# A written-out matmul order made anew on a plan that also counts GpSimd and the readiness of split weights: one adaLN transformer block on one Trainium2 core

## The chip, the cores and the metric

The kernel runs on one core of one Trainium2 chip. The metric is the device time of one execution in microseconds (us); for the kernel before it is 2359.66 us, the median of three executions.

The engines are named as in the profile: PE is TensorE (PEld its weight loads), DVE is VectorE, ACT is ScalarE, POOL is GpSimd, SP is SyncE, which here issues all DMAs (SPq in the rows).

## The reference

One transformer block over a sequence of 2048 rows of 576 numbers, 32 heads of 18, feed-forward width 4608, all in fp32. Six vectors of 576 come from a conditioning vector `c`:

```python
mod = (silu(c) @ w_mod).reshape(1, 6, 1, -1)          # sa, ca, ga, sb, cb, gb
h = layernorm(x) * (1 + ca) + sa
q, k, v = heads(h @ wqkv)
p = softmax(q @ k.T * 18 ** -0.5)
x = x + ga * ((p @ v) @ wo)
h = layernorm(x) * (1 + cb) + sb
x = x + gb * (silu(h @ w1) @ w2)
```

## The kernel before

**Arithmetic.** Each fp32 factor of a projection is split into a high part and a low part, both in a rounded fp32 type that TensorE takes in one pass. A product is then three products: high by high, high by low, low by high (`PASS`). Activations are split as they are made; the weights `wqkv`, `wo`, `w1`, `w2` are split once. Splitting costs a copy (the high part, `w[:, 1]` in `split_half`, L728) and a subtraction (the low part, `w[:, 0]`, L744), both on GpSimd, and for `wo` and `w2` a multiplication by the gate `ga` or `gb` before it (L740).

**Stages.** A first part (scheduled by the class `Start`, not touched here) normalises x and makes the first queries, keys and values. Then comes the attention loop over four query blocks of 512 rows (`NQB`), each with eight groups of four heads ("quads"), each quad with 64 *slots*. One slot is two matmuls that share the PE array, one in each half of its rows: `psa` (L851), whose row maxima DVE takes (L853, the tile `mx`), and `psb` (L903), whose exponential ACT takes (L905, the tile `pt`). `psa` runs 40 double slots ahead of `psb` (`LEAD`), since the maxima have to be there. After the slots of 128 keys follow the value products `psv` (L940), eight matmul records of the trace for each such step. There are 2048 slots and 512 value steps in all.

**Fill.** Whatever else PE has to do is put between slots as *fill*, piece by piece (class `Filler`). While query block 0 runs, fill is the rest of the query and key projections (`psqk`, L632). When the last value step of block b is through, `post(b)` (L1007) makes the fill that runs beside the slots of block b+1:

- the output projection `psp`, four row tiles of 56 matmuls (lines L513 and L519), with the attention output split into `th` and `tl` (`o_T`, L1024 to L1032) as one factor and the split `wo` as the other;
- the addition to x (`add_x1`, L1053 on DVE, L1056 and L1057 by way of ACT and GpSimd) and the second layer norm (L1063 to L1081, with a power on GpSimd at L421);
- the transposes `psT` of the normalised rows `ob` (`h_T`, L1091), followed by ACT (`etmp`, L439), DVE (`hh`, L442) and GpSimd (`hl`, L446);
- 36 tiles of `w1` in 18 pairs (`mlp1`, 54 matmuls a pair: `ps<-hh,w1t`, `ps<-hl,w1t`), the SiLU (L1181 to L1191, whose low part `g` is made on GpSimd), and 36 tiles of `w2` in 9 rounds of four (`mlp2`, 192 matmuls a round: `ps<-w2t,g`), with another `add_x1`.

For b = 0 the weights of `post` are loaded raw and split as they are needed, in halves of a tile: `load_half` (L717) issues the DMA into one of three buffers `raw`, `split_half` (L728) issues the GpSimd work, and a finished tile is stored to DRAM, from where blocks 1 to 3 load it split. For b = 3 there are no more slots, and the fill runs alone.

**What sets the order.** PE's instructions stand in the order in which the program issues them; the other engines' order is made by the compiler's own scheduler, except that some instructions (`after_pe`, L491) are tied to the latest `psb`: among them the `raw` loads and the first instruction of each split. PE's order is the string `ORDER`, one letter a decision: `s` is a slot, `f` one piece of fill, a digit so many value steps. The main loop (L1650 on) reads it beside a plan of time (class `Plan`, L133): `plan.t` is the time at which PE is thought to be, `plan.op` puts an operation on a queue of ACT ("A") or DVE ("V") with a length in ns, `chain` a row of them, and `plan.ring`, `take` and `when` say when a PSUM buffer is thought free. Where the next letter is not yet possible by the plan, the plan's clock moves on by 20 ns and nothing is issued. So the plan doesn't wait on the chip: it only decides at which letter the loads, splits and layer-norm steps are issued, and which orders are possible at all. Three modes of PE are told apart in it (`half`: slots and fill in halves of the rows; `full`; `values`), with a charge for each change of mode.

GpSimd has no queue in this plan. What waits for it is guessed: the low parts of the attention output by a time (`o["th"]`, at + 1500), the low part of the SiLU by at + 1600, the normalised rows by at + 900, the readiness of split weights not at all: `proj`, `mlp1` and `mlp2` only ask for two free PSUM buffers (`pair_need`, L462). A `raw` load is issued when fewer than three halves are waiting to be split (`serve`, L753).

Of the kernel before, what the change touches and what calls it, by code (L numbers as in the profile page):

```python
# [25 lines left out]
KT = 5  # L26
# [14 lines left out]
CH = 4  # L41
# [20 lines left out]
    "sssfsssfsssfsss1sss1sssfsssfsssfss1sss1sss1sss1sss1sss1sss1sss2sssfsssfsssfsss1sss1sss1sss1ss1sssfsss2sssffsss"  # L62
    "1sssfsssfsssfsss1sss1sss1sss1sss1sss2sssffsssfsss1sss1sss1sss1sss1ss1sssfsss11sssffsss1sssfsssfsssfsss1sss1sss"
    "1sss1sss1ss1sssfsssffsss1sss1sss1sss1sss1sss1ss1sss1sssffffsssffsssfsssfsss1sss1sss1sss1sss1sss1sss1ss1sss1sss"
    "fffsssfsss1sss1sss1sss1sssf1sss1sssfsssffsss1sss2sssffsssfsssfsss1sss1sss1sss1sss1sss1ssffsssffsss1sss1sss1sss"
    "1sss1sssfffsssfsss1sss1sssf1sssfffsss1sss1sss1sss1sss1sssfffsssfsss1sss1sss1sss2sss1sssf1sss1sss1sssfsssfsssfs"
    "ss1sssfsss2sssffsss1sss1sss1sss1sss1ssfsssfsssfsss1sss1sss1ss2sssfsssfsssfsss1sss1sss1sss1sssfsss2sssffsss1sss"
    "1sss1sssfsssfsss1sss1sss1ssssfss1ss1ss1ss1ss1ssssssssssss1ss1ss1ss1fss1fss1ss1ssss1ssssssfffs1ssffsfsffffssfff"
    "sffffssffsfffffsfffffffss1fffffffssfffffffss1fffffffsfffffffss13sfffssffs1sffssffsfsffssffsfsfsfsffs3sfsfffsfs"
    "ffsfsfsfsfsfsffs2sfsfsffsfsffssffsfsfsfsfsfs13ssffsffssffsfsfs1ssffsffssffsfsfs1ssffsffssffsffss2ssffsffssffsf"  # L70
    "fss3ssffsfsfsfsffssffsfsfsfsffs3sfffsfsfsffssffsfsfsfsffs4sffsffssffsffss1ssffsffssffsffss21ssffsffssffsffss1s"
    "sffsffssffsfsfs2ssffsfsfsfsffssffsfsfsfsffss4ssffsfsfsfsffssffsfsfsfsfsfs1sfsfff3ssffsffss1ssffsffssffsfsfs1ss"
    "ffsffssffsffss2ssffsffssffsfsfs3ssffsfsfsfsffssffsfsfsfsfsfs13ssffsfsfsfsffssffsfsfsfsfsfs1sffffssfffsfs1sfsff"
    "fssffsffs3ssffsffssffsffss1sfsfsffssffsffss3ssffsfsfsfsffssffsfsffsffs3sfsfsffsfsffssffsfsfsfsffs4sfsfsffssffs"
    "fsfs1ssffsffssffsfsfs1sfsfffssffsffss2sfsfsffssffsffss3ssffsfsfsfsffssffsfsfsffsfs4ssffsfsfsfsffssffsfsfsfsfsf"
    "s22ssffffssffsffss1ssffsffssffsffss1ssffsffssffsfsfs1sfsfffssffsffss4ssffsfsfsfsffssffsfsfsfsffss3ssfffssffsff"
    "ssffsfsfsfsfsfs22ssffsffssffsffss1ssffsffssffsfsfs12ssffsffssffsffss1sfsfffssffsffs2ssffsfsfsfsffssffsfsfsfsff"
    "ss3ssfffssffsffssffsfsfsfsffss4ssffsffssffsfsfs1ssffsffssffsfsfs3ssffsffssffsffss1ssffsffssffsffss1ssffsfsfsfs"
    "ffss1sfsfss2ss1ss1ss1sffff1ffffsfsfsfsfs1ssffsffssffsfsfs1ssfffsfsffsfs1ssfffsfsffsfs1ssffsffssffsffss1fffffff"
    "ssfffffffss1fffffffssfffffffss1fffffffssfffffff1sffsffssffffss2sff2fs1ssffsfffsffssffsfsfsfsffs2sfsfsffsfsffss"  # L80
    "ffsfsfsfsfsfs3ssfffssffsffssffsfsfsfsfsfs13ssffffssffsffss1ssffsffssffsffss2ssffsffssffsffss1ssffffssffsfsfs3s"
    "sffsfsfsfsffssffsfsfsfsfsfs3ssfffssffsffssffsfsfsfsfsfs4ssffsffssffsffss1ssffsffssffsfsfs1ssffsffssffsfsfs4ssf"
# [26 lines left out]
GP = [range(i, i + 2) for i in range(0, 28, 2)]  # L109
MMC = 228  # L110
MMH = 131

TS, TV, TX, TL, TR = 228, 858, 100, 430, 60
TMAX, TEXP = 605, 495
TLAT = {"A": 100, "V": 85}


def head_rows(h):

    kt, r0 = divmod(DH * h, P)  # L120
    n = min(P - r0, DH)
# [252 lines left out]
def tile_adaln_block(ctx: ExitStack, tc: tile.TileContext, x, wqkv, wo, w1, w2, c, wfirst, wcol, out):  # L374
# [331 lines left out]
    def weights(key, make, n, src, scr, first, gate=None, hold=None):  # L706

        if not first:
            nc.sync.dma_start(f(make()), f(scr))
            return  # L710
# [1016 lines left out]
```

## Time and profile before

| | |
|---|---|
| time, median of 3 (lowest to highest) | 2359.66 us (2354.22 to 2360.62) |
| the profiled execution: its own time | 2358.8 us |
| its span, first to last instruction | 2356.2 us |
| first `psb` of query block 0, 1, 2, 3 | 155.8, 546.0, 1070.5, 1572.6 us |
| end of the last `psb` | 2077.4 us |
| PE busy | 2286.8 us |
| DVE busy | 1775.4 us |
| POOL busy | 711.9 us |

How to read it: the profile shows one execution. Its own time is 2.6 us more than its span, and 0.9 us less than the median. The rows of the table with `psb` say in which stretch of the span a query block's slots run: `post(0)`, with the splitting of `wo`, `w1` and `w2`, runs from 546 to about 1070 us. A busy PE isn't a PE at its peak: the record of a matmul also holds the time in which it is only passing through, and the clock that it was granted can be half.

### The profile page before, as it was taken

Reading aid. Unit: us, or ns where it says so; the run is one execution under the profiler, and the core shown is the slowest. Engines: PE = TensorE matmul, PEld = TensorE weight load, DVE = VectorE, ACT = ScalarE, POOL = GpSimd, SP = SyncE. Lnnn points to the kernel's source line nnn. Section 1 sums busy time; section 2 is a strip of 40 time slices with the busy share of each in tenths; the row PEclk is TensorE's granted clock in tenths of the full one; section 3 lists DMA queues with packets and bytes.
Section 4 is the critical chain, followed back from the end, with each engine's and each line's share of the span. In section 5 each row is a group of like instructions: output and inputs, shape, how many; then the busy total and the mean of one; then the engine's idle time right before and its main releaser. Section 6 shows DMA issues by size and latency. Waiting matters only on the chain.

```text
span 2356.2 us, 52136 instructions
## 1 busy us (share of the span) xinstructions
PE 2286.8 (97%) x19844; PEld 1579.9 (67%) x19844; DVE 1775.4 (75%) x3089; ACT 1470.7 (62%) x2710; POOL 711.9 (30%) x873
## 2 busy tenths in 40 slices
PE   5999999999799999999999999999999999999999
PEld 4884444444476766776767677677676777678998
DVE  7769898887688888888888888787888778244333
ACT  4237777776377777777577777676777677732221
POOL 5113323315646666665211111112211111210000
PEclk9999999998899999999999999999999999999999
DMA  7465555546456666676555545554655554345653
GB/s 250 153 196 172 167 170 167 175 154 204 146 203 207 216 211 226 228 229 213 203 175 176 181 173 166 163 188 140 218 170 165 194 187 151 132 150 197 221 201 114
DMA packets 201474, 433.01 MB, mean 184 GB/s; under 512 B 31362, under 2 KB 67618, under 8 KB 201226
## 3 DMA queue, kind: packets, MB, share of 16 engines
q1 hardware_dynamic: 201226, 429.68, 55.0%
q8 instruction: 158, 2.59, 0.5%
q14 instruction: 90, 0.74, 0.1%
HBM read 338.54 MB, written 86.33 MB: 180 GB/s over the span
## 4 chain that ended last, share of the span: by engine, by line
PE 85%; DVE 6%; DMA 3%; POOL 2%; issue 1%; ACT 1%; SPq 0%; ACTq 0%; DVEq 0%; POOLq 0%
PE ps L519 26%; PE psv L940 18%; PE psa L851 14%; PE ps L513 10%; PE psb L903 8%; PE psqk L632 3%; DVE mx L853 3%; PE psv L519 2%; PE psp L519 1%; PE psqk L519 1%; PE psv L1420 1%; PE psqk L1420 1%; PE psp L513 1%; DMA vt<-vscr 1%; DMA raw<-in_w 1%
## 5 line engine op out<-in xcount | busy, mean ns | idle before, releaser
L853 DVE TENSOR_REDUCE mx<-psa 128x1 f32<-128x512 f32 x2048 | 1329.8, 684 | 282.5 <-PE psb L903 167.4
L905 ACT ACTIVATE pt<-psb 128x512 f32<-128x512 f32 x2048 | 1142.6, 599 | 471.4 <-PE psb L903 317.5
L903 PE MATMUL psb<-qt,kb 56*128 56x512 f32 x2048 | 740.0, 421 | 2.8 <-ACT pt L905 2.8
L851 PE MATMUL psa<-ka,qt 54*128 54x512 f32 x2016 | 729.6, 418 | 10.8 <-DVE mx L853 8.4
L851 PEld LDWEIGHTS psa<-ka,qt 54*128 54x128 f32 x2016 | 344.5, 186 | 314.2 <-DVE mx L853 200.9
L940 PE MATMUL psv<-pt,vt 128*32 128x512 f32 x4096 | 505.2, 601 | 0.0
L519 PE MATMUL ps<-w2t,g 64*128 64x288 f32 x4992 | 407.3, 292 | 2.5 <-POOL w2t L744 1.7
L519 PEld LDWEIGHTS ps<-w2t,g 64*128 64x128 f32 x4992 | 383.4, 185 | 30.9 <-ACT etmp L1187 2.5
L519 PE MATMUL ps<-hh,w1t 64*128 64x512 f32 x1944 | 360.8, 396 | 8.0 <-POOL w1t L743 5.4
L903 PEld LDWEIGHTS psb<-qt,kb 56*128 56x128 f32 x2048 | 350.3, 186 | 24.3 <-ACT pt L905 12.8
L1191 POOL TENSOR_TENSOR g<-etmp,g 128x512 fp32r<-128x512 f32 x108 | 138.3, 1300 | 392.8 <-ACT g L1190 312.7
L940 PEld LDWEIGHTS psv<-pt,vt 128*32 128x32 f32 x4096 | 102.0, 109 | 207.5 <-issue 201.2
L519 PEld LDWEIGHTS ps<-hh,w1t 64*128 64x128 f32 x1944 | 200.4, 188 | 52.3 <-POOL w1t L743 6.3
L1057 POOL TENSOR_TENSOR x<-x,gt 128x288 f32<-128x288 f32 x116 | 93.0, 802 | 382.5 <-ACT gt L1056 382.5
L519 PE MATMUL ps<-hl,w1t 64*128 64x512 f32 x864 | 181.6, 394 | 0.0
L1053 DVE TENSOR_TENSOR x<-ps,x 128x288 f32<-128x288 f32 x184 | 83.5, 454 | 110.5 <-PE ps L513 71.5
L513 PE MATMUL ps<-w2t,g 128*128 128x288 f32 x960 | 130.8, 296 | 2.9 <-POOL g L1191 1.4
L513 PEld LDWEIGHTS ps<-w2t,g 128*128 128x128 f32 x960 | 128.6, 188 | 5.6 <-POOL g L1191 1.9
L1187 ACT ACTIVATE eq<-ps 128x512 f32<-128x512 f32 x36 | 21.5, 598 | 146.4 <-PE ps L513 146.4
L513 PE MATMUL ps<-hh,w1t 128*128 128x512 f32 x360 | 106.9, 390 | 0.5 <-DVE hh L448 0.5
L519 PEld LDWEIGHTS ps<-hl,w1t 64*128 64x128 f32 x864 | 91.4, 188 | 15.7
L1188 DVE SCALAR_TENSOR_TENSOR etmp<-etmp 128x512 f32<-128x512 f32 x108 | 75.8, 740 | 14.0 <-ACT etmp L1187 13.6
(150 smaller groups left out, 2137.8 us busy)
## 6 DMA issues: line engine op xcount, KB each, us to landing
w1t<-w1s SPq DMA_DIRECT2D x108, 640.0 KB
w2t<-w2s SPq DMA_DIRECT2D x108, 576.0 KB
kb<-kscr SPq DMA_DIRECT2D x512, 108.0 KB
ka<-kscr SPq DMA_DIRECT2D x504, 108.0 KB
w1s<-w1t SPq DMA_DIRECT2D x36, 640.0 KB
w2s<-w2t SPq DMA_DIRECT2D x36, 576.0 KB
vt<-vscr SPq DMA_DIRECT2D x32, 608.0 KB
qt<-qscr SPq DMA_DIRECT2D x128, 108.0 KB
```

The lines of the kernel that those rows point to most:

```text
L513: mm(self.ps[late], lhsT=lhsT, rhs=rhs, start=(i == 0), stop=(i == self.n - 1))
L519: done = mm(self.ps[g], lhsT=lhsT[rows], rhs=rhs[rows], start=(s == 0), stop=(s == self.end))
L632: mm(qk_ps[0], lhsT=w[b][:, kt, :], rhs=(hTl if a else hTh)[:, kt, n * 512:(n + 1) * 512], start=(i == 0), stop=(i == 13))
L851: mm(ps, lhsT=t["q"][64 * j:64 * j + 54, hp, stt * P:(stt + 1) * P], rhs=t["a" if ("a", kc, hp) in t else "b", kc, hp][64 * j:64 * j + 54, ...
L853: return lambda: nc.vector.tensor_reduce(t["mx"][:, 2 * j + hp, stt, kc:kc + 1], ps, axis=AX.X, op=ALU.max)
L903: state["pe"] = mm(ps, lhsT=t["b", kt // 4, hp][64 * e:64 * e + 56, kt % 4 * P:(kt % 4 + 1) * P], rhs=t["q"][64 * e:64 * e + 56, hp, :], s ...
L905: nc.scalar.activation(t["P"][kt, hp][:, e, :], ps, AF.Exp, scale=SCALE)
L940: mm(t["ps"][32 * h:32 * h + 32, :], lhsT=t["v"][:, c0:c0 + 32], rhs=t["P"][kt, h // 2][:, h % 2, :], start=(kt == 0), stop=(kt == NKT - 1 ...
L1053: nc.vector.tensor_add(c["x1"][j][:, hs], ps, c["x1"][j][:, hs])
L1057: nc.gpsimd.tensor_add(c["x1"][j][:, hs], c["x1"][j][:, hs], t)
L1188: nc.vector.scalar_tensor_tensor(t, t, 1.0, u, op0=ALU.add, op1=ALU.mult)
L1191: (nc.vector if last else nc.gpsimd).tensor_tensor(g[:, 1, :], t, f(g[:, 0, :]), op=ALU.subtract)
```

## The change

The plan gets a third queue, "G" for GpSimd, and the operations that were guessed are put on it with lengths: 3100 for the column sums of `col_dot`, 1560 for the low part of a projection weight, 1900 for the parts of a `qk` output, 1360 (`GW1`) for half a `w1` tile, 2080 (`GW2`) for half a `wo` or `w2` tile, 1290 or 1900 for the low parts of the attention output and of the normalised rows, 810 for the addition to x, 560 for the power, 1300 for the low part of the SiLU. A small class `Event` lets one step of the layer norm wait in the plan for the one before it. New conditions say when fill may start: a projection when all of `th` and all split `wo` are thought ready, a `w1` pair when its two tiles and (the first pair) all normalised low parts are, a `w2` round when its four tiles are. A `raw` load now waits for a `raw` buffer that is thought free (a ring of three, released when the split is thought through), and a piece of the gate vectors (`mod_piece`) for a free PSUM buffer. The string `ORDER` is replaced. No instruction that computes is added, removed or altered.

```diff
-    "sssfsssfsssfsss1sss1sssfsssfsssfss1sss1sss1sss1sss1sss1sss1sss2sssfsssfsssfsss1sss1sss1sss1ss1sssfsss2sssffsss"
...
+    "sssfsssfsssfsss1sss1sss1sss1sss1ss1sssfsssfsssfsss1sss1sss1sssfsssffsss1sss1sss1sss1sss1sss2sss1sssfffsss1sssf"
...
-TLAT = {"A": 100, "V": 85}
+TLAT = {"A": 100, "V": 85, "G": 60}
+GW1, GW2 = 1360, 2080
...
-        self.free = {"A": 0, "V": 0}
-        self.queue = {"A": [], "V": []}
+        self.free = {"A": 0, "V": 0, "G": 0}
+        self.queue = {"A": [], "V": [], "G": []}
...
-        flight.append((plan.t, ask, h, raw))
+        flight.append((plan.t, ask, h, raw, plan.take("raw")))
...
+        def done(at):
+            rel(at)
+            if h:
+                split[key] = at + 100
+        plan.op("G", plan.t, GW1 if ask["gate"] is None else GW2, done)
...
-        if asks and len(flight) < 3 and last_load[0] + EACH[asks[0]["gate"] is not None] <= plan.t:
+        if asks and plan.is_ready(plan.when("raw")) and last_load[0] + EACH[asks[0]["gate"] is not None] <= plan.t:
             load_half()
+
+    def all_ready(*ats):
+
+        return None if any(at is None for at in ats) else max(ats, default=0)
+
+    def weights_need(*keys):
+
+        return all_ready(*[split[key] for key in keys if key in split])
...
-            chain([("A", 780), ("V", 430)], plan.t, plan.take("f"))
+            c["hT", kt] = None
+            chain([("A", 780), ("V", 800), ("G", 1290 if kt < 4 else 1900)], plan.t, plan.take("f"), lambda at: c.update({("hT", kt): at + 100}))
...
         def o_need():
-            at = pair_need()
-            return None if at is None or o["th"] is None else max(at, o["th"])
+            return all_ready(pair_need(), *[c.get(("th_at", kt)) for kt in range(KT)], weights_need(*[("wo", kt) for kt in range(KT)]) if b == 0 else 0)
...
         def hT_need():
-            at = bank_need()
-            return None if at is None or ("ln_at", 3) not in c else max(at, c["ln_at", 3])
+            return all_ready(bank_need(), c["ln", 3].at) if ("ln", 3) in c else None
...
+            def first_need():
+                ats = [c.get(("hT", kt)) for kt in range(KT)] if i == 0 else []
+                return all_ready(pair_need(), *ats, weights_need(("w1", i), ("w1", i + 1)) if b == 0 else 0)
```

What the new string does to PE's order, counted from the two orders, over the first 128 slots of query block 1 (the slots numbered 512 to 639; a fill is named by the slot before it):

| | before | now |
|---|---|---|
| first `psp` matmul after slot | 543 | 549 |
| last `psp` matmul after slot | 559 | 585 |
| transposes `psT` after slot | 562 and 564 | 589 |
| first `ps<-hh,w1t` after slot | 566 | 603 |
| first `ps<-w2t,g` after slot | 603 | 638 |
| matmuls with `w1t` up to slot 639 | 190 | 162 |
| matmuls with `w2t` up to slot 639 | 192 | 24 |
| matmuls with `w1t` / `w2t` up to slot 1023 | 918 / 1488 | 918 / 1440 |
| changes of mode in the whole loop | 747 | 753 |

Query block 0 (slots 0 to 511) keeps its fill, at other slots, with 349 changes of mode before and 347 now. The first part of the program is the same.

The first place is PE's row where the projection of block 0 begins; `psp<-wo` are the projection's matmuls (each number after `wo` is one tile of weights), `psa` and `psb` together a slot. Before:

```order
L851 MATMUL psa<-ka_81,qt 128x512
L903 MATMUL psb<-qt,kb_85 128x512
L519 MATMUL psp<-wo_6857,th 128x288 x4
L519 MATMUL psp<-wo_6857,tl 128x288 x2
L519 MATMUL psp<-wo_6918,th 128x288 x2
L851 MATMUL psa<-ka_81,qt 128x512
L903 MATMUL psb<-qt,kb_85 128x512
```

And now:

```order
L890 MATMUL psa<-ka_82,qt 128x512
L942 MATMUL psb<-qt,kb_86 128x512
L539 MATMUL psp<-wo_6861,th 128x288 x4
L539 MATMUL psp<-wo_6861,tl 128x288 x2
L539 MATMUL psp<-wo_6922,th 128x288 x4
L539 MATMUL psp<-wo_6922,tl 128x288 x2
L890 MATMUL psa<-ka_82,qt 128x512
```

The first matmul of the projection has moved six slots back (the key tiles are those of the next chunk, `ka_82` for `ka_81`).

The second place is PE's row from the transposes `psT` to the first products with `w1t`. Before:

```order
L1091 MATMUL psT<-ident,ob 128x128 x8
L851 MATMUL psa<-ka_80,qt 128x512
L903 MATMUL psb<-qt,kb_88 128x512
L940 MATMUL psv_7057<-pt_2031,vt_2039 32x512 x2
L940 MATMUL psv_7057<-pt_2032,vt_2039 32x512 x2
L851 MATMUL psa<-ka_80,qt 128x512
L903 MATMUL psb<-qt,kb_88 128x512
L519 MATMUL ps_7863<-hh,w1t 128x512
```

And now, from the transposes on:

```order
L1142 MATMUL psT<-ident,ob 128x128 x20
L890 MATMUL psa<-ka_83,qt 128x512
L942 MATMUL psb<-qt,kb_84 128x512
L890 MATMUL psa<-ka_83,qt 128x512
L942 MATMUL psb<-qt,kb_85 128x512
L890 MATMUL psa<-ka_83,qt 128x512
L942 MATMUL psb<-qt,kb_85 128x512
L890 MATMUL psa<-ka_80,qt 128x512
L942 MATMUL psb<-qt,kb_86 128x512
L979 MATMUL psv_7955<-pt_2036,vt_2040 32x512 x2
```

Two slots and one value step stood between the last transpose and the first product with `w1t`; now it is 14 slots and three value steps, of which the first four slots and the first rows of a value step are shown.

149 lines of the change are left out of this document (89 added, 60 removed).

## The prediction

> **What bounds the kernel now.** I read the page first, then PE's waits, then the stages, then the rows of the stage that stands out. A difference of 0.3% (7 us) is about what a measurement of this kernel can tell from no change.
>
> From the page, the totals, and PE's busy tenths with its granted clock in 40 slices of 58.9 us:
>
> ```profile
> span 2356.2 us, 52136 instructions
> ...
> PE 2286.8 (97%) x19844; PEld 1579.9 (67%) x19844; DVE 1775.4 (75%) x3089; ACT 1470.7 (62%) x2710; POOL 711.9 (30%) x873
> ...
> PE   5999999999799999999999999999999999999999
> ...
> PEclk9999999998899999999999999999999999999999
> ```
>
> PE is the bound, and its matmuls are the same before and now. So the time can only come out of its gaps and of its clock. Both dip at one place past the start: the 11th slice (589 to 648 us) has a 7, and the 10th and 11th a clock of 8. That is where query block 1 begins and `wo`, `w1`, `w2` are split for the first time.
>
> PE's waits by line and releaser, over the span (total, times, longest):
>
> ```profile
> PE psT L1354 <- ACT xt L1346: 20.1, 8, 17.6
> ...
> PE psT L1091 <- DVE ob L435: 6.0, 2, 4.9
> PE ps L519 <- POOL w1t L743: 5.4, 2, 4.2
> ...
> PE psp L519 <- POOL tl L1030: 2.5, 2, 2.3
> PE psm L589 <- DVE mx L853: 2.1, 8, 0.3
> PE ps L519 <- POOL w1t L744: 1.8, 2, 1.2
> ...
> PE ps L519 <- POOL w2t L744: 1.7, 2, 1.5
> ```
>
> The first is the start, which the change leaves alone. The waits for `ob` (the norm), `w1t`, `tl` and `w2t` are the ones that the new plan counts: 17.4 us if all of them went.
>
> The stages, by windows (length, busy time with count of PE, PEld, DVE, ACT, POOL; then granted clock, DMA): query block 0 from 177 us; the first 128 slots of block 1; its other 384; the first 128 slots of block 2.
>
> ```profile
> 176.72:530.14 353.42, 350.24 (x2200) 154.08 (x2202) 317.51 (x556) 263.97 (x513) 111.00 (x127) 1.00 0.53 167
> 545.97:703.80 157.83, 138.25 (x1138) 91.20 (x1139) 112.98 (x203) 88.80 (x161) 96.45 (x135) 0.88 0.56 187
> 703.80:1070.51 366.71, 363.70 (x3584) 254.28 (x3580) 310.48 (x502) 267.10 (x488) 236.59 (x321) 1.00 0.66 217
> 1070.51:1207.10 136.59, 134.15 (x1308) 92.34 (x1304) 113.74 (x210) 93.45 (x172) 51.68 (x61) 1.00 0.60 200
> ```
>
> The second and fourth rows are the same stage of two blocks. With the same slots and the same DVE work (113 us), block 1 takes 157.83 us for 1138 matmuls and block 2 136.59 us for 1308. Block 1 has 19.6 us of idle PE (157.83 - 138.25) and a mean clock of 0.88. The clock is either whole or half, so half-speed time is 2 x 0.12 x 157.83 = 37.9 us. What both cost together is at most 19.6 + 37.9 / 2 = 38.5 us, less whatever idle time lies inside the slow stretches.
>
> **The change, part by part.**
>
> *The four stalls at the start of block 1.* PE's rows there (start, length, in brackets the idle time before and what ended it):
>
> ```profile
> 576.59 0.48 PE L519 MATMUL psp<-wo,tl 64*128 64x288 f32 x2 [2.26 <-POOL tl L1030]
> ...
> 613.99 1.33 PE L1091 MATMUL psT<-ident,ob 128*128 128x128 f32 x5 [4.95 <-DVE ob L435]
> ...
> 626.58 0.80 PE L519 MATMUL ps<-hh,w1t 64*128 64x512 f32 x2 [4.22 <-POOL w1t L743]
> 628.61 0.79 PE L519 MATMUL ps<-hh,w1t 64*128 64x512 f32 x1 [1.24 <-POOL w1t L744]
> ```
>
> Each is an order that came too early: the piece stood in PE's row before its input could be there, and the slots behind it, which needed nothing of it, stood still with DVE and ACT. The new order starts the projection six slots later, spreads it over 36 slots instead of 16, and puts 14 slots and three value steps between the transposes and the first `w1t` product. From the transposes (613.99) to the end of the `w1t` waits (628.61) the chain took 14.6 us here. A slot needs one reduction on DVE, 685 ns by the next row, so the 14 slots alone last at least 9.6 us, and the five conversions that DVE makes for the normalised rows are 5.6 us more: 15.2 us, about what the chain needs. So I expect these waits to go nearly whole, with a rest of a microsecond or two.
>
> DVE's rows in the first 128 slots of block 1: the reductions and these conversions.
>
> ```profile
> L853 DVE TENSOR_REDUCE mx<-psa 128x1 f32<-128x512 f32 x129 | 84.0, 685 | 31.7 <-PE psa L851 15.3 <-PE psb L903 8.9 <-PE ps L519 6.5
> L442 DVE CAST hh<-etmp 128x512 fp32r<-128x512 f32 x5 | 5.6, 1123 | 1.0 <-ACT etmp L439 1.0
> ```
>
> *What becomes the bound there.* With fill taken out of the 128 slots, DVE is late next. PE's part first, worked out from block 2's window by taking away the fill that the new order doesn't have there. Fill costs, by starts of rows in a dense stretch:
>
> ```profile
> 2064.97 1.75 PE L519 MATMUL ps<-w2t,g 64*128 64x288 f32 x24
> 2066.56 0.40 PE L903 MATMUL psb<-qt,kb 56*128 56x512 f32 x2
> ...
> 2075.61 0.64 PE L519 MATMUL ps<-hh,w1t 64*128 64x512 f32 x4
> 2076.07 0.40 PE L519 MATMUL ps<-hl,w1t 64*128 64x512 f32 x2
> ```
>
> 24 matmuls with `w2t` take 1.59 us (66 ns each) and 4 with `w1t` 0.46 us (115 ns each). Block 2's window has these fills:
>
> ```profile
> L519 PE MATMUL ps<-hh,w1t 64*128 64x512 f32 x144 | 28.0, 394 | 0.4 <-POOL hh L448 0.4
> L519 PE MATMUL ps<-w2t,g 64*128 64x288 f32 x328 | 27.1, 294 | 0.8 <-POOL g L1191 0.8
> ...
> L519 PE MATMUL ps<-hl,w1t 64*128 64x512 f32 x64 | 14.1, 391 | 0.0
> ...
> L519 PE MATMUL ps<-h,w1t 64*128 64x512 f32 x8 | 2.1, 402 | 0.0
> ```
>
> That is 216 with `w1t` and 328 with `w2t`; the new order has 162 and 24 there. 54 x 0.115 + 304 x 0.066 = 26.3 us less, so PE would need 110 us. DVE's work stays 113 us. So DVE sets the pace, and the question is how full it can get. Its densest long stretch is block 0, 317.51 of 353.42 us, 90%: 113 / 0.90 = 125.6 us. Were it always busy: 113 us.
>
> The fill that the new order leaves for later than the old one is 28 x 0.115 + 168 x 0.066 = 14.3 us; it is made up by slot 1023 (48 matmuls short, 3 us) in stretches where PE is the bound, so it costs its full time. Stage and debt: 127.3 to 139.9 us against 157.83, a gain of 17.9 to 30.5 us. I take 20, near the lower end, because 90% is what the trace shows over hundreds of microseconds and because not every wait will go; the upper end serves the range.
>
> *The rest of block 1* has 366.71 - 363.70 = 3.0 us of idle PE, of which the wait for `w2t` is 1.7. I take 1.5, bounds 0 and 3. *The pieces `psm`* wait eight times, 2.1 us together, for a PSUM buffer; the plan now asks for it first. I take 1.5, bounds 0 and 2.1. *The same stages of blocks 2 and 3* have little to give: block 2's window has 136.59 - 134.15 = 2.4 us of idle PE. I take 1 for both, bounds 0 and 4.
>
> *Changes of mode*: 753 for 747. Two slots between two value steps start 0.34 us apart:
>
> ```profile
> 562.05 0.50 PE L851 MATMUL psa<-ka,qt 54*128 54x512 f32 x1
> ...
> 562.39 0.40 PE L851 MATMUL psa<-ka,qt 54*128 54x512 f32 x1
> ```
>
> Two half-array matmuls over 512 columns, which is what a slot is, take 0.23 us in the dense rows above. At the 0.11 us between these, six more changes are 0.7 us lost; at three times that, 2.
>
> *What else moves.* In SP's queue a `raw` load waits for its buffer (in all, times, longest):
>
> ```profile
> SPq L722 <- POOL w2t L744: 69.6, 27, 6.1
> ```
>
> Behind these 69.6 us of waits stand the loads of keys for the slots. The new condition issues a load when the buffer should be free, so most of this should go. I cost it at nothing, since no wait of PE above is for a key load; if the keys were near their limit it could only help.
>
> Sum: 20 + 1.5 + 1.5 + 1 - 0.7 = 23.3 us. The profiled execution took 2358.8 (span 2356.2 and 2.6 around it), so 2335.5; the median stands 0.9 higher: 2336. With all upper bounds the gain is 30.5 + 3 + 2.1 + 4 = 39.6 (2320); with the lower ones 17.9 - 2 = 15.9 (2344).
>
> **A rule of the skill against the trace.** Five windows of block 1's start, three before the first long stall and two at the last:
>
> ```profile
> 540.00:545.00 5.00, 4.75 (x30) 1.81 (x23) 4.25 (x8) 3.75 (x8) 0.00 (x0) 1.00 0.76 245
> 545.00:550.00 5.00, 5.00 (x15) 3.17 (x14) 4.75 (x8) 3.92 (x8) 0.64 (x1) 0.61 0.95 320
> ...
> 555.00:560.00 5.00, 4.62 (x34) 1.10 (x26) 4.55 (x9) 4.67 (x10) 2.69 (x6) 1.00 0.72 233
> ...
> 625.00:630.00 5.00, 2.19 (x8) 1.44 (x10) 0.00 (x0) 0.00 (x0) 4.31 (x6) 0.50 0.25 82
> 630.00:635.00 5.00, 5.00 (x26) 3.81 (x24) 2.52 (x4) 2.09 (x4) 0.00 (x0) 0.52 0.78 290
> ```
>
> After the stall at 626.58 the clock is half, and DVE and ACT, at 0.00, have nothing. But in the second row it is 0.61 in a stretch of slots and value steps where PE counts as busy throughout and after a window with 0.25 us of idle, while in the third, a like stretch, it is whole. So a thin stretch can lose its clock without a long gap, and the new order has more thin stretches; this is the third rival. The Trainium skill's page "TensorE: Matmul & The Clock Gate" (Part 1) says that the clock falls to half after an idle window of about 3.4 us, and advises no gap over that. The second row doesn't agree: no gap of that length comes before it. By the page only the stalls of 4.95 and 4.22 us would have cost clock, the third rival would fall away, and the sum would stay as it is.
>
> **The rivals.**
>
> *The waits move on (16%).* GpSimd's own order is made by the compiler's scheduler, not by the plan, so a split can still stand behind another operation there. For it: GpSimd worked 96.45 us of the 157.83, so its queue is what counts. Against it: the new lengths lie close to the trace's. If half of the stage's gain is kept: 2358.8 - 13 + 0.9 = 2347.
>
> *The plan doesn't fit the chip (12%).* The new order shifts the stalls to other pieces, and nothing measurable is left: 2353 to 2366, say 2358. For it: the old plan was wrong by whole microseconds at four places. Against it: each of these four is one that the old plan didn't count.
>
> *The thin stretch runs at half clock (3%).* From slot 549 to 603 PE has the projection and little else; at 125.6 / 128 us a slot these 54 slots last 53 us. For it: the second of the five windows. Against it: the third. Half clock over all of it would cost at most half of it, 26 us, less what DVE's pace hides: 2362. It takes the whole gain away from 46 us of half clock, where this block's start has 37.9 now.
>
> *The supply of split weights becomes the bound (6%), the slower case.* Loads and splits now go by the plan's buffer ring. GpSimd's first operation of a `w2` split, in block 1 from slot 128 on:
>
> ```profile
> L740 POOL TENSOR_TENSOR raw<-raw,gb 128x288 f32<-128x288 f32 x54 | 44.2, 823 | 74.4 <-DMA raw<-in_w 26.7 <-PE psb L903 20.4 <-PE psa L851 19.0
> ```
>
> The plan holds a buffer for `LAND` (6 us) and a split (2.08), so three give a half every 2.7 us; 144 halves must pass in some 450 us, 3.1 each. For it: the 26.7 us that GpSimd waited for landings show that 6 us isn't always enough. Against it: POOL is busy 236.59 of 366.71 us. If the cycle took 10.1 us instead of 8.1, a half would take 3.4, 0.25 too long, and 144 of them 36 us: 2336 + 36 = 2372. It is slower than before by more than 0.3% from a cycle of 9.9 us.
>
> *More than I count* (2%): 2315, if the new order is also better in blocks 2 and 3.
>
> **How the numbers follow.** The forecast, 2336, has 61%, with 2320 to 2346 as its own range. Faster by over 0.3%: 61 + 16 + 2 = 79%. Within 0.3%: the second and third rivals, 12 + 3 = 15%. Slower: the fourth, 6%. The range reaches past the first rival and a little into the second: 2320 to 2354.
>
> **What would show it.** Right: in the first 128 slots of block 1 the four waits for `tl`, `ob` and `w1t` shrink from 12.7 us to under 3, the stage's DVE share rises from 72% towards 90%, it takes 122 to 130 us, and the clock there is above 0.93. SP's waits for POOL ahead of `raw` loads fall by more than half. Wrong: a stage above 145 us, waits for `w1t` or `w2t` above 8 us in the whole span, or the clock below 0.9 in the thin stretch.

## The result, and the profile after

| | time, median (lowest to highest) | ratio to before, 95% interval |
|---|---|---|
| before | 2356.94 us (2352.24 to 2360.62), 6 runs | |
| after | 2375.28 us (2370.06 to 2380.09), 6 runs | 1.0076 [1.0055, 1.0096] |

The changed kernel is slower by 0.8%, about 18 us, where 2336 us was forecast. Its profiled execution took 2376.84 us, with a span of 2375.1. From its page:

```profile
span 2375.1 us, 52137 instructions
...
PE 2296.8 (97%) x19844; PEld 1580.5 (67%) x19844; DVE 1767.2 (74%) x3089; ACT 1476.1 (62%) x2710; POOL 713.4 (30%) x873
...
PE   5999999999899999997999999999999999999999
...
PEclk9999999998899999997999999999999999999999
```

In slices of 59.4 us, the 11th slice of PE has an 8 where it had a 7. The clock keeps its two 8s there, and both rows have a new 7, in the 19th slice (1069 to 1128 us). That is the start of query block 2, where before had 9s. PE's waits over the span (total, times, longest):

```profile
PE psT L1409 <- ACT xt L1401: 20.1, 8, 17.6
PE ps L539 <- POOL w2t L775: 12.2, 3, 9.4
PE psa L890 <- DVE mx L892: 9.7, 14, 3.3
PE ps L539 <- POOL w2t L772: 7.6, 4, 5.6
...
PE psT L1142 <- DVE ob L455: 1.8, 2, 1.1
PE psp L539 <- POOL th L1075: 1.7, 1, 1.7
PE psp L539 <- POOL tl L1073: 1.0, 1, 1.0
```

The waits for `w1t` are gone, and those for `ob` and `tl` have shrunk from 8.5 to 2.8 us, as forecast. In their place stand 19.8 us for `w2t`, of which 5.6 and 9.4 are single waits. The 9.7 us for a row maximum are not new; before had 8.4:

```profile
PE psa L851 <- DVE mx L853: 8.4, 16, 2.8
```

The same three stages as before (length, busy time of PE, PEld, DVE, ACT, POOL; granted clock, DMA share, GB/s): the first 128 slots of block 1, the other 384, the first 128 of block 2:

```profile
543.59:685.00 141.41, 129.44 (x956) 76.84 (x957) 108.25 (x200) 87.98 (x158) 82.61 (x113) 0.89 0.57 185
685.00:1063.47 378.47, 373.49 (x3698) 264.43 (x3698) 311.00 (x504) 268.84 (x490) 251.24 (x343) 1.00 0.66 215
1063.47:1223.20 159.73, 139.64 (x1306) 94.54 (x1304) 112.13 (x209) 93.56 (x171) 49.84 (x61) 0.93 0.55 181
```

Against before the first is 16.4 us shorter, the second 11.8 longer, the third 23.1 longer: 18.5 of the span's 18.9 us. The first stage's gain is mostly work moved on: it has 956 matmuls for 1138, and the second has 3698 for 3584. The third has as many matmuls (1306 for 1308) and is simply slower: PE stands idle for 20.1 us (159.73 - 139.64), where it was 2.4, and the clock is 0.93, where it was 1.00.

**The third stage.** Both kernels end the last-but-one round of `w2` at 1074.0 us. After starts the last round (tiles 32 to 35) at 1090.65. PE's rows, in brackets the idle time before:

```profile
1072.25 1.77 PE L539 MATMUL ps<-w2t,g 64*128 64x288 f32 x24
...
1090.65 0.96 PE L539 MATMUL ps<-w2t,g 64*128 64x288 f32 x12
...
1097.62 0.61 PE L539 MATMUL ps<-w2t,g 64*128 64x288 f32 x2 [5.64 <-POOL w2t L772]
...
1107.67 0.84 PE L539 MATMUL ps<-w2t,g 64*128 64x288 f32 x3 [9.44 <-POOL w2t L775]
```

Counted from the end of the round before, it started 4.7 us later in before, and 22 matmuls went through at once:

```profile
1073.03 0.96 PE L519 MATMUL ps<-w2t,g 64*128 64x288 f32 x12
...
1095.32 1.92 PE L519 MATMUL ps<-w2t,g 64*128 64x288 f32 x22
1098.07 0.40 PE L519 MATMUL ps<-w2t,g 64*128 64x288 f32 x2 [0.83 <-POOL g L1191]
```

PE's order says where the 4.7 us went. In both kernels 1049 slots stand ahead of the last round. The round before it ends when 1029 slots have begun in before, and 1037 in after, since after still had 48 `w2` matmuls to make up at slot 1023. So 20 slots and eight value steps lay between the two rounds, and now 12 and six.

The splits of three of these tiles can only begin when the round before is over, since `w2` has five tile buffers. GpSimd's rows in after:

```profile
1096.29 0.79 POOL L771 TENSOR_TENSOR raw<-raw,gb 128x288 f32<-128x288 f32 x1 [2.90 <-DMA raw<-in_w]
1097.14 0.42 POOL L772 CAST w2t<-raw 128x288 fp32r<-128x288 f32 x1
1104.11 1.54 POOL L771 TENSOR_TENSOR raw<-raw,gb 128x288 f32<-128x288 f32 x2 [6.54 <-DMA raw<-in_w]
1105.60 1.26 POOL L1073 TENSOR_TENSOR tl<-ou,th 128x512 fp32r<-128x512 f32 x1
1106.82 0.79 POOL L775 TENSOR_TENSOR w2t<-raw,w2t 128x288 fp32r<-128x288 f32 x1
...
1110.76 1.54 POOL L775 TENSOR_TENSOR w2t<-raw,w2t 128x288 fp32r<-128x288 f32 x2
```

The low part at 1106.82 belongs to the high part at 1097.14, and PE's wait of 9.44 us ends with it (1107.61). GpSimd could have made it at 1097.6, but two multiplications stand ahead of it in its queue, which wait 6.54 us for the last two raw loads, and then a low part of the attention output (1.26 us). The last split is done at 1112.3, 38.3 us after the end of the round before. In before it was done at 1096.8, 22.8 us after it:

```profile
1095.99 0.80 POOL L744 TENSOR_TENSOR w2t<-raw,w2t 128x288 fp32r<-128x288 f32 x1
```

SP's rows show where the loads were. After, then before:

```profile
1084.92 4.64 SPq L1007 DMA_DIRECT2D ou<-ov  x5
...
1093.89 0.37 SPq L746 DMA_DIRECT2D raw<-in_w  x1
...
1097.59 1.03 SPq L746 DMA_DIRECT2D raw<-in_w  x2
```

```profile
1085.65 0.36 SPq L722 DMA_DIRECT2D raw<-in_w  x1
...
1091.22 5.02 SPq L968 DMA_DIRECT2D ou<-ov  x5
```

Before issued its last raw load ahead of the five DMAs of the attention output; after issued three behind them. Counted so in the other runs below, one load is behind all five in runs 1, 2, 3, 5, 9, 10 and 11, three are in 4, 7, 8 and 12, and none is in 6.

### The profile page after: what moved, and what is told of

Read it like the earlier page. It is cut to its first block, busy times and chain, and to the rows that moved or that the text cites. A ratio compares the mean times of both kernels' runs of the same rounds, so it can differ in the third digit from the quotient of the medians.

```text
span 2375.1 us, 52137 instructions
## 1 busy us (share of the span) xinstructions
PE 2296.8 (97%) x19844; PEld 1580.5 (67%) x19844; DVE 1767.2 (74%) x3089; ACT 1476.1 (62%) x2710; POOL 713.4 (30%) x873
## 4 chain that ended last, share of the span: by engine, by line
PE 87%; DVE 5%; DMA 3%; POOL 2%; ACT 1%; issue 1%; SPq 0%; DVEq 0%; ACTq 0%; POOLq 0%
PE ps L539 26%; PE psv L979 19%; PE psa L890 14%; PE ps L533 10%; PE psb L942 8%; PE psqk L654 4%; DVE mx L892 2%; PE psv L539 2%; PE psp L539 1%; PE psv L1475 1%; PE psqk L539 1%; DMA raw<-in_w 1%; PE psqk L1475 1%; PE psp L533 1%; DMA qt<-qscr 1%
## 5 line engine op out<-in xcount | busy, mean ns | idle before, releaser
L942 PE MATMUL psb<-qt,kb 56*128 56x512 f32 x2048 | 750.4, 422 | 3.8 <-ACT pt L944 3.7
L890 PEld LDWEIGHTS psa<-ka,qt 54*128 54x128 f32 x2016 | 350.3, 187 | 300.0 <-DVE mx L892 172.4
L539 PE MATMUL ps<-w2t,g 64*128 64x288 f32 x4992 | 419.5, 294 | 20.2 <-POOL w2t L775 12.2
L539 PEld LDWEIGHTS ps<-w2t,g 64*128 64x128 f32 x4992 | 389.0, 186 | 65.0 <-POOL w2t L775 14.8
L539 PE MATMUL ps<-hh,w1t 64*128 64x512 f32 x1944 | 352.9, 395 | 0.0
L539 PEld LDWEIGHTS ps<-hh,w1t 64*128 64x128 f32 x1944 | 194.4, 186 | 48.2 <-issue 5.0
L1238 DVE SCALAR_TENSOR_TENSOR etmp<-etmp 128x512 f32<-128x512 f32 x108 | 77.8, 759 | 13.1 <-ACT etmp L1237 12.3
```

The costliest lines, as they stand in the source:

```text
L539: done = mm(self.ps[g], lhsT=lhsT[rows], rhs=rhs[rows], start=(s == 0), stop=(s == self.end))
L890: mm(ps, lhsT=t["q"][64 * j:64 * j + 54, hp, stt * P:(stt + 1) * P], rhs=t["a" if ("a", kc, hp) in t else "b", kc, hp][64 * j:64 * j + 54, ...
L942: state["pe"] = mm(ps, lhsT=t["b", kt // 4, hp][64 * e:64 * e + 56, kt % 4 * P:(kt % 4 + 1) * P], rhs=t["q"][64 * e:64 * e + 56, hp, :], s ...
L1238: nc.vector.scalar_tensor_tensor(t, t, 1.0, u, op0=ALU.add, op1=ALU.mult)
```

## The experiments

All ratios are to before, run on the same chip. The stages are those of the three rows above, cut at the same slots. A piece of the string is told by the counts of slots `s`, of fills `f` and of value steps that stand ahead of it.

**1 to 3: the rule for loads and the string apart.** The change has two parts that reach PE: the new string, and the plan's new rule for when a raw load is issued. The first run puts the old rule back into the changed kernel:

```diff
-        if asks and plan.is_ready(plan.when("raw")) and last_load[0] + ...
+        if asks and len(flight) < 3 and last_load[0] + ...
```

> The changed kernel with one line put back: a raw load is issued when fewer than three halves wait to be split, not when the plan thinks a raw buffer free. The order of PE is the new one. Theory G (the gate): the new condition issues the last loads of w2 of block 0 later in SP's row, and that is why PE waits 9.4 + 7.4 us at the last w2 round, at the start of block 2. Then the wait at that place falls from 16.8 us to under 4, the clock there stays whole, and the time falls by 17 to 23 us against the changed kernel: ratio to the kernel before 0.996 to 1.001. Theory O (the order): the new string asks for these tiles too late in PE's row whatever the gate, since the condition of the last round counts no weights. Then the wait stays above 12 us and the ratio is 1.005 to 1.008.

Measured: 2372.32 us, 1.0056 [1.0033, 1.0078]. The second puts the new string into the kernel before, with nothing else of the change:

```diff
 ORDER = (
-    "sssfsssfsssfsss1sss1sssfsssfsssfss1sss1...
+    "sssfsssfsssfsss1sss1sss1sss1sss1ss1sssf...
```

> The kernel before with the new string alone: no GpSimd in the plan, the old conditions, the old gate. Theory G: no wait above 4 us at the last w2 round, ratio to the kernel before 0.995 to 1.001. Theory O: the wait at the last w2 round is above 10 us and the ratio at least 1.004. Both: the start of block 1 looks as in the changed kernel (waits for w1t and ob under 3 us together), since PE's row is nearly the same there.

Measured: 2372.19 us, 1.0058 [1.0039, 1.0077]. Its stages lie within 1.1 us of the first run's, so with the string given, all of the plan but the rule for loads hardly matters. The third puts the old string into the changed kernel (the same diff, turned round):

> The changed kernel with the old string: the new plan, gate and conditions, but PE's old row. Theory G: the old waits at the start of block 1 stay (over 10 us for tl, ob and w1t) and a wait of 8 to 17 us comes in at the last w2 round, ratio 1.005 to 1.010. Theory O: no new wait at the last w2 round, ratio 0.999 to 1.002.

Measured: 2376.71 us, 1.0085 [1.0055, 1.0116]. Either part alone makes the kernel about as slow as both together, so neither is the cause by itself. Both bring a wait to the same place. With the new string and the old rule PE waits 8.5 us for `w2t` in the last round (5.5, and 3.0 in two). With the old string and the new rule, PE's waits from 1060 to 1170 us begin:

```profile
PE ps L539 <- POOL w2t L775: 4.2, 2, 2.6
PE ps L539 <- POOL w2t L772: 4.1, 1, 4.1
```

With the new string and the old rule the rest of block 1 is 388.3 us, 10 longer than in after, and PE's waits from 690 to 1060 us begin:

```profile
PE ps L539 <- POOL w2t L775: 8.9, 3, 4.6
```

So with the new string the new rule cures waits in the middle of block 1 (3.0 us of `w2t` are left before 1060 us in after), and with either string it brings or lengthens the one at the start of block 2.

**4: the last round later.** The changed kernel, with 14 slots and two value steps moved ahead of the last round:

```diff
-    "ss1fffffffssss2ss1ss1fs1sfsfffffsff1sfsfsfsfs1ssffsffssffsfsfs1sfffssffffss...
+    "ss1fffffffssss2ss1ss1fs1sfsfffs1sssss1ssssssssf1fsffsffsffsffsffsffsffsffsf...
```

> The changed kernel with 14 slots and two value steps of the string moved ahead of the last w2 round, the rest of that stretch packed behind them; plan and gate are the new ones. 14 slots at 0.7 to 0.8 us are some 10 us of cover. Both theories: the wait of 16.8 us falls to 5 to 8, less clock is lost, and the time falls by 8 to 15 us against the changed kernel, ratio 1.001 to 1.004. If the wait stays above 14 us, the loads are not late by the clock but stand behind something in SP's row that moves with PE, and both theories lack it.

Measured: 2368.05 us, 1.0033 [1.0020, 1.0047]. The long waits for `w2t` are gone (3.1 us for the low part in the span, the longest 1.9), and the start of block 2 falls from 159.7 to 150.3 us, not to 137.

**5 and 6: the two strings cut and joined** at their common place, 1049 slots, 651 fills and 261 value steps, in the kernel before. New up to there and old from there:

```diff
-    "sssfsssfsssfsss1sss1sssfsssfsssfss1sss1...
+    "sssfsssfsssfsss1sss1sss1sss1sss1ss1sssf...
...
     "...ffff1ffffsfsfsfsfs1ssffsffssffsfsfs1ssfffs...
```

> The plan of before, with the new string up to the 1049th slot and the old one from there, so that the last round of second-layer weights stands as in before. Theory R (the loss belongs to where the new string puts the last round): the first 128 slots of block 1 take 133 us as in the run with the old plan and the new string, the start of block 2 comes down from 151 to about 137 us, and the time is about 2358 us, ratio 1.000. Theory S (the new string empties the queues' slack in block 1 and the round is late wherever it stands): the waits for w2t stay above 12 us, the start of block 2 stays near 150 us, and the time is about 2370 us, ratio 1.005.

Measured: 2427.97 us, 1.0300 [1.0280, 1.0319]: neither theory's time. The start of block 2 takes 178 us, and the rest of it 401 us, in every other run 365 to 367; in the span PE waits 12.4 us for `etmp` and 12.6 for `x`, most of it in block 2. The old string's tail doesn't fit this start, so the time tells nothing about the last round. Its rows do. The round has the old letters here and stands behind the new block 1, with 12 slots since the round before as in after. By the two clocks of experiments 9 to 11 its last split is 15.4 us late, and PE waits 11.1 us in it for `w2t`, most of it for high parts:

```profile
PE ps L519 <- POOL w2t L741: 8.0, 2, 4.7
```

Now old up to there and new from there:

```diff
-    "...ss1ss1ss1sffff1ffffsfsfsfsfs1ssffsff...
+    "...ss1ss1ss1ssff1sfsfsfsfs1ssffsffssffs...
```

> The plan of before, with the old string up to the 1049th slot and the new one from there. Theory R: the first 128 slots of block 1 take 158 us as in before, the start of block 2 takes about 150 us with over 10 us of waits for w2t, and the time is about 2370 us, ratio 1.005. Theory S: nothing presses on the loads, the waits for w2t are below 3 us, and the time is 2356 to 2360 us, ratio 1.000.

Measured: 2365.45 us, 1.0030 [1.0019, 1.0041]. 3.0 us of waits for `w2t` are left, none of them in the last round, whose last split is done 2.2 us before the round starts. The start of block 2 takes 141.3 us with 60 matmuls less in it. What follows from both: the new string's last round is not late by its own letters; it is late behind the new block 1. That is theory S, though the time isn't back at 2358.

**7 and 8: what holds the loads in SP's queue.** SP's waits in after between 540 and 1120 us, at the write-back of split weights (L782) for the split and at raw loads (L746) for a buffer:

```profile
SPq L782 <- POOL w2t L775: 49.0, 22, 7.5
...
SPq L746 <- POOL w2t L775: 18.5, 14, 3.5
...
SPq L746 <- POOL w1t L775: 15.8, 12, 2.3
```

First the write-back goes to GpSimd's own queue:

```diff
-        nc.sync.dma_start(f(scr), f(w))
+        nc.gpsimd.dma_start(f(scr), f(w))
```

> The changed kernel, with the split weights written back by GpSimd's queue in place of SyncE's; the order of TensorE is the same. Theory Q (the write-back waits for its split at the head of SyncE's queue, up to 7.5 us, and holds the loads behind it): SyncE's waits at the write-back vanish (49.0 us for w2t between 540 and 1120 us), TensorE's waits for w2t fall from 19.8 us to below 8, the start of block 2 falls from 160 to about 145 us, and the time falls by 10 to 15 us, to about 2362. Rival B (the transfers themselves are slow, or the ring of three buffers holds the loads): the waits for w2t stay above 15 us and the time at 2372 to 2378. A third reading: GpSimd pays for each write-back itself and the time rises above 2380.

Measured: 2376.57 us, 1.0092 [1.0066, 1.0118]. SP's wait at the write-back is gone, but the one at the raw load has grown from 18.5 to 36.7 us, and PE's waits for `w2t` stay:

```profile
SPq L746 <- POOL w2t L775: 36.7, 22, 4.2
...
PE ps L539 <- POOL w2t L775: 12.1, 6, 8.1
...
PE ps L539 <- POOL w2t L772: 4.9, 3, 3.2
```

Neither theory Q's time nor its waits came; the table below has 3.5 us of lateness less from this edit. Then a fourth raw buffer (a 48-byte statistics tile goes from three buffers to two to make room):

```diff
-        raw = mp["p"].tile([P, 320], F32, tag="raw", name="raw", bufs=3)[:, :n]
+        raw = mp["p"].tile([P, 320], F32, tag="raw", name="raw", bufs=4)[:, :n]
```

> The changed kernel with a fourth buffer for raw weights on the chip, while the plan still counts three (and two buffers in place of three for a 48-byte statistics tile, to make room); the order of TensorE is the same. Rival B (the ring holds the loads): SyncE's waits at the raw load for GpSimd's split (18.5 and 15.8 us between 540 and 1120 us) vanish, TensorE's waits for w2t halve to 10 us or less and the time falls by 5 to 12 us. Theory Q (the write-back at the head of the queue holds them): SyncE's waits at the write-back take the place, TensorE's waits for w2t stay above 15 us and the time stays within 3 us of 2375.

Measured: 2370.19 us, 1.0050 [1.0033, 1.0067], with 20.3 us of waits for `w2t`. SP's wait moves from the raw load to the write-back (69.5 us there), as theory Q said, and PE's stays. The time is 5 us below after's, as rival B had it, but not through these waits: the start of block 2 takes 161.3 us, and shorter are the first 128 slots of the profiled run (135.3 us, within their spread of 133 to 145). Neither a buffer alone nor the write-back alone makes the last loads late. Each run only moved SP's wait to the other place, and both changes in one kernel were not run. The place of the loads in the order of issue, behind the attention output, is tried in experiment 10.

**9 to 11: two clocks.** What is left is a race. One clock runs from the end of the last-but-one round to the end of the last split. The other runs from there to the first matmul of the last round. Both are read for each run from the same rows as above. The late split is one number less the other:

| run | last split after | round starts after | late by | start of block 2 |
|---|---|---|---|---|
| before | 22.8 | 21.3 | 1.5 | 136.6 |
| 3, old string, new rule | 30.1 | 21.2 | 8.9 | 145.4 |
| 1, new string, old rule | 29.4 | 17.1 | 12.3 | 149.6 |
| 2, new string, plan of before | 31.5 | 17.3 | 14.2 | 150.7 |
| 7, write-back by GpSimd | 35.4 | 17.2 | 18.2 | 154.9 |
| after | 38.3 | 16.6 | 21.7 | 159.7 |
| 8, four raw buffers | 40.1 | 17.3 | 22.8 | 161.3 |

The stage grows by 1.1 to 1.2 us for each microsecond that the split is late. For the last split, the string is 6.6 us (run 1 less before), the rule 7.3 (run 3 less before), and both are 15.5, a little over their sum; the string also starts the round 4.7 us sooner. Three runs were foretold from this. Old rule for all loads, and the round 14 slots later (the edits of 1 and 4):

> The changed kernel with the old rule for loads and with the last round of second-layer weights 14 slots later. If the loss at block 2's start is a race between two clocks (when the last split is done, counted from the end of the round before: 22.8 us in before, 29.4 with the old rule and the new string, 38.3 in the changed kernel; and when the round starts: 21.3, 17.1 and 16.6 us), then the last split stays at about 29 us, the round starts at about 32 us, TensorE's waits for w2t in the round vanish (below 2 us there), the start of block 2 takes 138 to 142 us instead of 149.6, and the time falls by about 9 us from the 2372 of the old rule alone, to about 2363. Rival: the round is late for another reason (transfers crowded at block 2's start), the waits move to the next rows and the time stays at 2368 to 2374.

Measured: 2366.72 us, 1.0042 [1.0029, 1.0055]; last split after 31.3 us, start after 28.2, start of block 2 145.9 us. There is no wait for `w2t` from 1060 to 1180 us; PE's waits there begin:

```profile
PE psb L942 <- ACT pt L944: 1.7, 4, 0.9
PE psp L539 <- DVE x L1096: 1.1, 2, 0.8
```

The time fell by 5.6 of the 9 us expected, or 3 by the ratios, whose intervals overlap, so a gain isn't shown; the start of block 2 is 3.7 us shorter than in run 1. Then the new rule everywhere but for the last four tiles:

```diff
-        if asks and plan.is_ready(plan.when("raw")) and last_load[0] + ...
+        if asks and (len(flight) < 3 if asks[0]["key"] >= ("w2", 32) and asks[0]["key"][0] == "w2" else plan.is_ready(plan.when("raw"))) and last_load[0] + ...
```

> The changed kernel with the old rule for the loads of the last four w2 tiles alone. By the two clocks: the last split is done about 30 us after the end of the round before in place of 38.3, the round starts at about 17 us as it did, so the waits for w2t fall by about 8 us, from 20 to about 12, and the time by 8 to 12 us, to about 2365. Rival (the rule for loads matters elsewhere, not at the last round): no change from 2375.

Measured: 2366.88 us, 1.0048 [1.0033, 1.0062]; last split after 32.6 us, start after 17.1, late by 15.5, start of block 2 153.8 us: on the table's line. PE's waits from 1060 to 1170 us have fallen from 16.8 to 10.9 us, and the time by 8.4 (about 7 by the ratios, whose intervals just overlap):

```profile
PE ps L539 <- POOL w2t L772: 7.8, 2, 4.7
PE ps L539 <- POOL w2t L775: 3.1, 2, 2.6
```

Both together:

> Both together: the old rule for the last four w2 tiles alone, and the last round 14 slots later. By the two clocks no wait for w2t above 1 us is left in the last round, the start of block 2 takes about 140 us, and the time is that of the round moved alone (2368) less 5 to 10 us: 2358 to 2363, no more than the kernel before. Rival: the net gain of the new string in the first part of block 1 shows at last, 2350 to 2355, below the kernel before. Second rival: 2368 as with the round moved alone.

Measured: 2363.9 us, 1.0027 [1.0015, 1.0039]. No wait for `w2t` is left in the round, but the start of block 2 takes 149.3 us, not 140. Two windows of it (columns as in the stages), the second just ahead of the round:

```profile
1082.00:1092.00 10.00, 9.26 (x66) 3.38 (x64) 7.27 (x10) 7.04 (x13) 9.17 (x13) 1.00 0.73 231
1092.00:1107.00 15.00, 12.87 (x48) 6.42 (x47) 10.31 (x16) 10.06 (x19) 12.30 (x14) 0.67 0.78 252
```

The slots moved there run without fill, and in that stretch the clock falls to half (0.67 over 15 us). So in this run moving the round trades a wait for a thin stretch at half clock. Half clock lasts 13.7 us here and in run 4, but only 3.4 in run 9, whose stage is long all the same: by what their splits are late, the three lie 7 to 13 us above the table's line. In runs 4 and 11 the half clock begins within 0.3 us of the end of a wait of PE for ACT's `pt` (1.75 and 1.89 us). In run 9, with the string of run 11, the longest wait there is 0.88 us, and the moved slots keep the whole clock. That points to the wait, and not to the thin stretch alone, but no run tried it. No run beat before.

**12: the first 128 slots.** The changed kernel, in which DVE stood 2.15 us behind GpSimd's addition to x:

```profile
599.51 0.46 DVE L1109 BATCH_NORM_STATS2 st<-x 128x6 f32<-128x288 f32 x1 [2.15 <-POOL x L1103]
```

```diff
+            if done is not None and b == 0:
+                nc.vector.tensor_add(c["x1"][j][:, hs], ps, c["x1"][j][:, hs])
+                return
             t = pool.tile([P, HH], F32, tag="gt", name="gt", bufs=2)
             nc.scalar.activation(t, ps, AF.Copy)
```

> The changed kernel; in block 0's projection the second half of each sum into x is added by VectorE from the accumulator itself, as the first half is, in place of a copy by ScalarE and an addition by GpSimd (the plan still counts the old chain, so TensorE's order is the same). In the first 128 slots of block 1 VectorE stood 2.15 us at the norm's second half, behind GpSimd's addition, which stood behind two splits, and TensorE waited 3.31 us for a row maximum. Theory V (such stands of VectorE on GpSimd make the waits that stayed in the first 128 slots): TensorE's waits for the row maximum there fall from 5.4 to about 2 us, the idle time of that stage from 11.7 to about 8, and the stage is 4 to 8 us shorter by what it is without them (137 us, the mean of the runs with this order there). Rival: VectorE is simply short of time there (108 of 141 us busy); four more additions of 0.45 us leave the waits at 5 us or more, and the stage at 135 to 145 us. The wait at the last round, 17 to 20 us, stays under both, and so the time stays within 2365 to 2376.

Measured: 2372.7 us, 1.0069 [1.0053, 1.0084]. PE's wait for the row maximum in that stage, in after and in this run:

```profile
PE psa L890 <- DVE mx L892: 5.4, 5, 3.3
```

```profile
PE psa L890 <- DVE mx L892: 3.2, 4, 1.2
```

The long wait is gone, but the idle time of the stage falls only from 12.0 to 9.7 us. That is a little over half of what theory V asked. The stage takes 134.1 us, which proves little: with the same string there it was 133 to 145 us in eleven profiled runs.

## Why the prediction was wrong

**The first 128 slots: the step that failed is the one that made DVE the pace.** It took DVE's 113 us at 90%, 125.6 us, and set PE's 110 us aside as shorter. After shows 108.25 of 141.41 us, 77%. PE's part was about right at full clock, but half clock was left out of it. At a clock of 0.89, half-speed time is 2 x 0.11 x 141.41 = 31.1 us, which costs 15.6 if none of it is hidden. Then 141.41 - 129.44 = 12.0 us of PE stood idle. 141.4 - 15.6 - 12.0 = 113.8 us remain, 3.8 more than the 110 that I had worked out. The profiled runs with the new string there bear that price out roughly: with 17.1 us of half clock the stage took 133.2 to 135.3 us (four runs), with 30.7 us 141.4 (after), with 37.5 us 145.2 (run 7). The four waits went as forecast, but 12 us of small ones (the row maximum 5.4, `th` 2.2, and others) stayed or came, and the clock rose from 0.88 to 0.89, not above 0.93. I had counted half clock as an effect of the stalls. For the most part it isn't: they went, and 17 to 38 us of it stayed in the eleven profiled runs with the new string there, where the three with the old string have 27 to 38. So the stage gave 16.4 us, and with the debt of 14.3 us about 2 of the 20 forecast. The eleven give 133 to 145 us: a net gain of 10 us at best, a loss of 2 at worst.

**The rest of block 1** was to be 1.5 us better. It is 11.8 longer, of which 11.3 is the debt at the prediction's prices (14.3 less the 3 still short at slot 1023), and PE idles 5.0 us where it idled 3.0.

**`psm`, and the starts of blocks 2 and 3.** The waits of `psm` are gone (2.1 us). Block 3's first 128 slots took 137.8 us for 139.7, a little better as forecast. Block 2's, forecast a little better, are the loss: 23.1 us. This is the larger failure, and the sign that the prediction had named for being wrong (over 8 us of waits for `w2t` in the span). The term that failed is "1 for both, bounds 0 and 4": it was read off the idle time of block 2's window in before (2.4 us) and had no loss in it. It did not ask by how much the splits had been early. They were 1.5 us late already by the table's clocks, with no wait of PE for `w2t` in that round, since the round takes its tiles one after another. A stage with no wait was taken for one with room. And the 48 matmuls still short at slot 1023 were priced as 3 us of PE alone; they also took 8 of the 20 slots between the last two rounds.

**"I cost it at nothing ... it could only help"**, on SP's queue, is the second step that failed. SP's wait at the raw load for `w2t` fell by more than half, as forecast. But it wasn't free: the new rule makes the last split 7.3 us later with the old string (experiment 3), and three raw loads stand behind the attention output's DMAs with it and the new string, for one with the old rule. With the old rule for just four tiles the kernel is about 7 us faster (experiment 10).

**The slower rival** (6%, 2372 us) named the cause in kind, split weights that come too late, and its time was near. Its working was wrong, so that its time was near is luck: it asked for a steady shortage over 144 halves, 0.25 us each. There was none (the waits for `w2t` before 1060 us are 3 us); the shortage came once, at eight halves, in a round whose own start condition doesn't ask for its tiles. In both kernels that condition is

```python
left[0] = left[0][:3] + (lambda: max(pair_need(), *c["gs"]) if pair_need() is not None and len(c["gs"]) == 2 else None,) + left[0][4:]
```

So the plan that now "counts the readiness of split weights" doesn't count it at the one place where it binds. Had the condition been written out in the prediction, this rival would have had its place.

**The thin stretch at half clock** (3%) was right too in part: the clock is half for 13.65 us, from 633.98 to 647.63. Two windows of it:

```profile
635.00:640.00 5.00, 5.00 (x22) 2.05 (x18) 5.00 (x8) 2.88 (x5) 4.54 (x5) 0.50 0.16 50
640.00:645.00 5.00, 5.00 (x24) 1.40 (x16) 2.28 (x4) 1.68 (x3) 0.45 (x1) 0.50 0.41 113
```

DVE is busy throughout the first, so there the half clock needn't cost anything. The rule of the Trainium skill's page "TensorE: Matmul & The Clock Gate" (Part 1), half clock after an idle window of about 3.4 us, doesn't cover these, as it didn't cover the window shown in the prediction: from 620 to 648 us no wait of PE is above 0.7 us.

**What stays open.** After the two cures of experiment 11, some 7 us against before are left. Its half clock at the moved slots, 13.7 us, would cost about as much, but run 9 has only 3.4 us of it and is no faster, so this is argued, not shown. With the old string and the new rule the rest of block 1 is 10.5 us longer: PE idles 8.0 us there for 3.0, mostly for `w2t` (7.2 us for 1.7), and 10.2 us of half clock would cost 5 more; why the rule brings these waits was not followed up. That the last loads are late by their place in SP's queue rests on experiments 3 and 10 and on the count of loads behind the attention output; a kernel that moves those DMAs alone was not run.

## What to carry to other kernels

When work is moved out of a stage, look for the stage that takes it in: measure there not the waits but the slack, as the time from the last input's arrival to its first use, since a wait of zero says nothing of the room behind it. A plan's rule is only as good as the one step that is exempt from it, so read each start condition on the path. And price a stretch of few matmuls at the clock that the trace grants to such stretches, not at full clock.

## What was not expected of the hardware

PE's clock can fall in stretches of slots without fill, with PE counted as busy (0.50 from 635 to 645 us in after, PE 5.00 of 5.00 in both rows). In the traces' clock records the half-clock stretches inside the span come in multiples of 3.41 us (3.4, 6.8, 10.2, 13.7, 17.1, 23.9). With one and the same order of PE the first 128 slots of block 1 had 17 to 38 us of half clock from run to run and took 133 to 145 us, while each stage of slots from the rest of block 2 on repeats within 0.4 us (run 5 left out, whose order is another there).

GpSimd's queue, which the compiler's scheduler fills, made the low part of a tile whose high part was done wait behind multiplications whose data had not landed (6.54 us); PE waited 9.44 us for it.
